# Block-sparse attention with two expert layers on one core: the first batch's attention drains in three steps, four output tiles are begun between them, and the token weights are made early

## The chip, the cores and the metric

The kernel runs on one core of a Trainium2 chip. The metric is the device time of one execution in microseconds (us), the median of several runs. Engines: PE is TensorE (its weight loads stand apart as PEld), DVE is VectorE, ACT is ScalarE, POOL is GpSimd, SP is the sync engine, which issues every DMA of this kernel.

## The reference

```python
# attention: q, k, v are [2, 8, 576, 64]; heads 0-3 see the last 32 positions, heads 4-7 see
# the earlier positions with the same remainder modulo 32
scores = scale * q @ k.T, masked to -1e9; attn = softmax(scores); attn_out = attn @ v
x = attn_out.transpose(0, 2, 1, 3).reshape(1152, 512)
# first expert layer: p = domain_probs / (domain_probs.sum(-1) + 1e-9), 4 experts, d_ff 1024
x = sum over e of p[:, e] * (relu(x @ w1[e]) @ w2[e])
# second layer, d_ff 1536, with weights in float64
out = (sigmoid(x @ w_gate) * (x @ w_val)) @ w_out
```

## The kernel before

**Attention** is cut into 32 groups, 16 for each of the two batches: 8 strided groups ("s", heads 4-7) and then 8 local ones ("l", heads 0-3). The text calls the first batch's groups 0 to 15 and the second's 16 to 31. A group passes through stages, one after the other: `scores` (TensorE, a mask product `sps` and the products of k and q into a score bank), `exp` (VectorE takes the negated maximum `nm`, ScalarE makes the exponentials `P` with their sums `sm`), `norm` (two small VectorE instructions on `sm`, then a multiplication of `P` on GpSimd), `transpose` (TensorE `tps`, VectorE copy `PT`), `values` (TensorE `o`, for two groups together) and `split` (the result is cut into a rounded part `xh` and a rest `xl`, the inputs of the next layer). `STAGES` says how many steps behind its scores a stage of a group stands: norm 1, transpose 3, values and split 5 (some 6). A step of `attention()` issues what falls on it, always in the order values, transpose, scores, exp, norm, split. All engines run their instructions in the order in which the program issues them.

The first batch's scores take steps 0 to 15. `DRAIN = 5` steps follow in which only its late stages are left, then the second batch begins at step 21. The first `FIRST_GROUPS = 21` steps run before the first expert layer; the steps after them are called from within its matrix products, 0.36 of a step for each product pair (`ATT_RATE`). In steps 12 to 20 the split reads the PSUM bank directly and VectorE makes both `xh` and `xl`; in other steps ScalarE copies the bank to `of` and GpSimd makes `xl` from that copy.

**Expert 0, "early"**: `early_up(s, T)` and `early_down(s, T)` work on 384 tokens in float32, each weight being split in two (`wh` by ScalarE, `wl` by GpSimd, one row of 128 each by `prep_early`, from a loaded tile `raw`), with three products for each pair. One call of `early_step` does one half of one such row, in this order: cast row, subtract row, and so on; the fifth call is the first on the item's second `raw` tile, the ninth ends an item. There are four items: up and down weights of the two halves of expert 0. `early_up(0, 0)` needs `xh` and `xl` of the first 384 tokens: rows 2 and 3 come from strided groups, rows 0 and 1 from local ones. `head_start(fb)` begins output tile `fb` of `early_up(0, 0)` with rows 2 and 3 (6 products); before the change that is done for tiles 0 and 1 in steps 17 and 18.

PSUM has four general banks (`gp`, "g"), three score banks (`sp_`, "s") and one for values (`op_`, "o"). `keep_warm(n)` issues n matrix products on zeros (`warm`), in the steps that `EMPTY` lists. `token_weights()` makes p from domain_probs on VectorE (in step 18); `spread_token_weights()` (step 19) transposes it on TensorE (`pps`), copies it out (`ptokT`), writes it to DRAM (`pd`) and reads it back spread over all partitions (`p00`). SP's queue is in the order of the program: the loads of later steps (`load_local(1)`, `load_strided_v(1, ...)`, `load_vl(1)`, `load_raw_to(n)`) stand behind one another.

After the early part come the experts 1 to 3 and the second layer, in float16 halves.

Of the kernel before, what the change touches and what calls it, by code (L numbers as in the profile page):

```python
# [9 lines left out]
F32 = mybir.dt.float32  # L10
# [24 lines left out]
WARM = 11  # L35
EMPTY = {0: 2, 1: 4, 2: 2, 3: 2, 4: 2, **{i: 2 for i in range(5, 16, 2)}, 16: 1, 19: 1, 20: 1}
T_BUFS = 4
# [9 lines left out]
QUAD = 4  # L47
FIRST_GROUPS = 21
PT_BUFS = 5
WEIGHTS_FROM = 12  # L50
DRAIN = 5
HEAD_START = (17, 18)
ATT_RATE = 0.36
# [53 lines left out]
def attn_moe_glu_kernel(ctx, tc, q, k, v, dp, w1, w2, wg, wv, wo, out):  # L107
# [20 lines left out]
    drp = ctx.enter_context(tc.tile_pool(name="drp", bufs=1, space=bass.MemoryType.DRAM))  # L128
    pd = drp.tile([NTB * E, 128], F32, tag="pd", name="pd")
    parked = {}  # L130
# [120 lines left out]
    zero = nc.const_aps.tensor(0.0, (128, 1), F32).bitcast(BF16)[:, 0:1]  # L251
    ptok = const.tile([128, NTB, E], F32, tag="ptok", name="ptok")
    psums = const.tile([128, NTB], F32, tag="psums", name="psums")
    SX = NI
# [35 lines left out]
    def token_weights():  # L290
        dve.tensor_reduce(psums, ptok, AX.X, ALU.add)
        dve.tensor_scalar(psums, psums, 1e-9, None, ALU.add)
        dve.reciprocal(psums, psums)
        dve.tensor_tensor(ptok, ptok, psums.unsqueeze(2).to_broadcast([128, NTB, E]), ALU.mult)

    def spread_token_weights():
        ps = gp.tile([128, 512], F32, tag="g", name="pps")
        nc.tensor.transpose(ps[:NTB * E, :128], ptok.rearrange("p t e -> p (t e)"), ident)
        t = atp.tile([128, 288], F32, tag="PT", name="ptokT", bufs=PT_BUFS)
        ptokT = t[:NTB * E, :128]  # L300
        dve.tensor_copy(ptokT, ps[:NTB * E, :128])
        nc.sync.dma_start(pd, ptokT)
        load_p(0, 0, p00)
# [3 lines left out]
    def load_p(e, T, t):  # L307

        m = TC // 128
        src = pd.rearrange("(t e) p -> e t p", e=E)[e, m * T:m * T + m, :]  # L310
        nc.sync.dma_start(t, bass.AP(src.tensor, src.offset, [[0, 128], [E * 128, m], [1, 128]]))
        pb[e, T] = t.rearrange("p a b -> p (a b)")
# [438 lines left out]
    def group_transpose(g):  # L751
        pp, _, n, w, m = soft.pop(g)
        ps = gp.tile([128, 512], F32, tag="g", name="tps")
        pv_ = ps[:w, :m * n].rearrange("p (a b) -> p a b", b=n)
        for j in range(m):
            nc.tensor.transpose(pv_[:, j, :], pp[:, j, :], ident[:n, :n])  # L756
        t = atp.tile([128, 288], F32, tag="PT", name="PT", bufs=PT_BUFS)
        tt = t[:w, :m * n].rearrange("p (a b) -> p a b", b=n)
        dve.tensor_copy(tt, pv_)
        pt_tiles[g] = tt  # L760

    def group_values(g):

        kind, b, c, half, hh = g
        if hh == 0:
            return
        if half and (kind, c) == ("l", 1):
            o = gp.tile([128, 512], F32, tag="g", name="o")
        else:
            o = op_.tile([128, 512], F32, tag="o", name="o")  # L770
        tts = [pt_tiles.pop((kind, b, c, half, x)) for x in range(2)]
        m, n = tts[0].shape[1], tts[0].shape[2]
        for j in range(m):
            for x in range(2):
# [7 lines left out]
                )  # L782
        if at_step[0] in range(WEIGHTS_FROM, FIRST_GROUPS):
            of_tiles[g] = o, o
            return
# [3 lines left out]

    def group_split(g):  # L790

        kind, b, c, half, hh = g
        if hh == 0:
            return
        o, of = of_tiles.pop(g)
        low = dve if of is o else pool_
        if kind == "s":
            kk = 2 + c
            hv, ov = (t[:, :288].rearrange("p (a u) -> p a u", u=NU) for t in (o, of))
            for T, off, s0, n in x_parts(b, 0, S):  # L800
                u0, u1 = s0 // 8, (s0 + n) // 8
                sel = lambda t: t[T][:, kk, off:off + n].rearrange("p (u a z) -> p z a u", a=4, z=2)[:, half]
                dve.tensor_copy(sel(xh), hv[:, :, u0:u1])
                low.tensor_tensor(sel(xl), ov[:, :, u0:u1], sel(xh).bitcast(F32), ALU.subtract)
        else:
            for T, off, s0, n in x_parts(b, 288 * half, 288 * half + 288):
                p0 = s0 - 288 * half
                dh, dl = xh[T][:, c, off:off + n], xl[T][:, c, off:off + n]
                dve.tensor_copy(dh, o[:, p0:p0 + n])
                low.tensor_tensor(dl, of[:, p0:p0 + n], dh.bitcast(F32), ALU.subtract)  # L810

    at_step = [0]

    def attention():
# [12 lines left out]
        step_of = [x + DRAIN * (x // (n // B)) for x in range(n)]  # L827
        at_stage = {}
        for name, behind in STAGES:
            for x in range(n):  # L830
# [6 lines left out]
                else:  # L837
                    at_stage[name, step_of[x] + behind] = gs[x]
        qk_strided(0, 0, (0,))
        for i in range(step_of[-1] + STAGES[-1][1] + 1):  # L840
            at_step[0] = i
            for name, _ in STAGES:
                if (name, i) in at_stage:
                    stage[name](at_stage[name, i])
            if i == 0:
                qk_strided(0, 0, (1,))
            if i in HEAD_START:
                head_start(HEAD_START.index(i))
            if i in EMPTY:
                keep_warm(EMPTY[i])  # L850
            for b in range(B):
                at = i - step_of[b * n // B]
                if b and at in (-5, -3):
                    qk_strided(b, 0, (int(at == -3),))
                if at in (2, 3):
                    qk_strided(b, 1, (at - 2,))
                if at in (6, 7, 9):
                    qk_local(b, (6, 7, 9).index(at))
            yield i
# [383 lines left out]
    with tc.manual_schedule():  # L1243
        load_strided_qk(0, 0)
        load_strided_qk(0, 1)
        warm_up()
        make_constants()
        load_local(0)
        load_strided_v(0, 0)
        load_strided_v(0, 1)  # L1250
        load_vl(0)
        nc.sync.dma_start(ptok, dp.rearrange("(t p) e -> p t e", p=128))
        for T in range(NT - 1):
            alloc_x(T)

        def attend():

            i = next(att, None)
            if i == 0:
                load_strided_qk(1, 0)  # L1260
                load_raw_to(2)
            if i == 6:
                load_raw_to(3)
                load_strided_qk(1, 1)
            if i == 9:
                load_strided_v(1, 0)
            if i == 11:
# [3 lines left out]
            if i == 18:  # L1271
                token_weights()
            if i == 19:
                spread_token_weights()
            if i == 20:
                load_vl(1)
# [3 lines left out]
        for i in range(FIRST_GROUPS):  # L1280
            attend()
            for _ in range((i >= WEIGHTS_FROM) + (i > 15)):
                early_step(0)
        n_none, n_step = 0, [0]
        halves = job(x_half())
# [21 lines left out]
        for n, u in enumerate(units):  # L1307
# [33 lines left out]
            for y in unit_steps(u):  # L1341
                if n < N_EARLY:
                    if y is None:
                        n_none += ATT_RATE
                        while n_none >= 1:
                            attend()
                            n_none -= 1
                        n_step[0] += 1
                        if n_step[0] % 2:
                            early_step(n)  # L1350
                elif y == "evac":
                    one_on()
# [36 lines left out]
```

## Time and profile before

| | us |
|---|---|
| median of 3 runs | 650.82 (650.52 to 651.32) |
| profiled execution | 651.06 |
| its span, first to last instruction | 648.9 |
| PE busy in the span | 638.2 (98%) |
| PEld, DVE, ACT, POOL busy | 469.3, 440.3, 341.7, 265.5 |
| granted TensorE clock, mean | 1.000 |

The span is 2.1 us shorter than the execution's time, which also holds what lies before the first and after the last instruction. A busy share counts the time in which an instruction of the engine runs; two instructions that overlap in the pipeline are counted once. Matrix products on zeros count as busy.

### The profile page before, as it was taken

The page shows a single profiled execution, that of the slowest core. Times are in us where ns is not written, and L with a number is a line of the kernel's source. Part 1 is how long each engine was busy: PE and PEld are TensorE (multiplying, and loading weights), DVE is VectorE, ACT ScalarE, POOL GpSimd, SP SyncE. Part 2 cuts the span into 40 slices and gives each one's busy share as a digit, 9 for nine tenths or more (in the row PEclk, how much of TensorE's full clock was granted, in tenths as well). Part 3 has the DMA queues.
Part 4 walks back from the last instruction along what each step waited for, and adds up shares of the span by engine and source line. Part 5 has one row for each costly group of instructions (what it writes and reads, how often), then busy time and mean ns, then how long its engine had stood idle before and what let it go on. Part 6 is the DMA issues. An engine that isn't in the chain of part 4 may idle for free.

```text
span 648.9 us, 12702 instructions
## 1 busy us (share of the span) xinstructions
PE 638.2 (98%) x4899; PEld 469.3 (72%) x4904; DVE 440.3 (68%) x885; ACT 341.7 (53%) x807; POOL 265.5 (41%) x307
## 2 busy tenths in 40 slices
PE   8889999999999999999999999999999999999998
PEld 5668889999676666666666666666979877987794
DVE  4876586787461886693887788898866659633432
ACT  5747553554854646774645554642565574532230
POOL 3665561000422226361335335440465377453540
PEclk9999999999999999999999999999999999999999
DMA  9965141030421544251664464354113832330002
GB/s 184 243 172 141 35 117 43 1 115 17 142 86 57 158 147 159 81 182 59 183 255 143 163 227 147 98 162 146 35 34 117 286 142 81 107 132 1 33 19 97
DMA packets 48884, 77.00 MB, mean 119 GB/s; under 512 B 19540, under 2 KB 24440, under 8 KB 47672
## 3 DMA queue, kind: packets, MB, share of 16 engines
q1 hardware_dynamic: 48824, 76.20, 37.6%
q8 instruction: 38, 0.62, 0.4%
q14 instruction: 22, 0.18, 0.1%
HBM read 59.66 MB, written 16.53 MB: 117 GB/s over the span
## 4 chain that ended last, share of the span: by engine, by line
PE 94%; DVE 1%; DMA 1%; SPq 1%; ACT 1%; issue 0%; POOL 0%; POOLq 0%; ACTq 0%
PE gps L874 23%; PE gps L876 23%; PE gps L875 23%; PE gps L976 19%; SPq L173 1%; PE sps L730 1%; PE warm L264 1%; PE tps L756 1%; PE o L780 1%; DMA ks<-in_k_dram 1%; ACT P L101 1%; DMA kl<-in_k_dram 1%; PE qkps L698 0%; PE qkps L676 0%; PE sps L717 0%; DVE nm L101 0%
## 5 line engine op out<-in xcount | busy, mean ns | idle before, releaser
L101 POOL TENSOR_TENSOR hl<-t,hh 128x384 f16<-128x384 f32 x72 | 76.5, 1065 | 179.2 <-ACT t L101 175.4
L976 PEld LDWEIGHTS <-w 128*128 128x128 f16 x1512 | 125.0, 98 | 1.8
L976 PE MATMUL gps<-x,w 128*128 128x192 f16 x1512 | 126.2, 246 | 0.0
L874 PE MATMUL gps<-x,w 128*128 128x384 f16 x288 | 93.9, 326 | 0.0
L875 PE MATMUL gps<-x,w 128*128 128x384 f16 x288 | 93.9, 326 | 0.0
L876 PE MATMUL gps<-x,w 128*128 128x384 f16 x288 | 93.9, 326 | 0.0
L874 PE MATMUL gps<-hh,w 128*128 128x384 f16 x288 | 93.9, 326 | 0.0
L875 PE MATMUL gps<-hl,w 128*128 128x384 f16 x288 | 93.9, 326 | 0.0
L876 PE MATMUL gps<-hh,w 128*128 128x384 f16 x288 | 93.9, 326 | 0.0
L874 PEld LDWEIGHTS <-w 128*128 128x128 f16 x576 | 56.4, 98 | 37.3 <-issue 0.2
L876 PEld LDWEIGHTS <-w 128*128 128x128 f16 x576 | 56.4, 98 | 37.2
L875 PEld LDWEIGHTS <-w 128*128 128x128 f16 x576 | 56.4, 98 | 36.4
L101 ACT ACTIVATE hh<-gps 128x384 f16<-128x384 f32 (+1 forms) x96 | 46.8, 487 | 48.8 <-PE gps L876 48.5
L101 POOL TENSOR_TENSOR stage<-magn,stage 128x512 f16<-128x512 f32 x36 | 45.5, 1273 | 45.1 <-ACT magn L101 38.9
L101 ACT ACTIVATE w<-raw,up 128x512 f16<-128x512 f32 x48 | 32.0, 715 | 34.8 <-DVE up L101 34.7
L101 ACT ACTIVATE P<-sps,nm 72x72 f32<-72x72 f32 (+1 forms) x112 | 36.4, 333 | 23.8 <-DVE sm L101 17.0
L101 ACT ACTIVATE bits<-raw 128x512 f32<-128x512 f32 x36 | 24.3, 674 | 38.1 <-DVE magn L101 37.9
L101 DVE SCALAR_TENSOR_TENSOR w<-raw,up,w 128x512 f16<-128x512 f32 x48 | 40.1, 871 | 5.1 <-ACT w L101 4.9
L101 POOL TENSOR_TENSOR sg<-four,sg 128x384 f32<-128x384 f32 x9 | 9.6, 1069 | 80.8 <-DVE four L101 77.9
L874 PE MATMUL gps<-w,hh 128*128 128x512 f16 (+1 forms) x112 | 41.6, 371 | 0.0
L875 PE MATMUL gps<-w,hh 128*128 128x512 f16 (+1 forms) x112 | 41.6, 371 | 0.0
L876 PE MATMUL gps<-w,hl 128*128 128x512 f16 (+1 forms) x112 | 41.6, 371 | 0.0
(145 smaller groups left out, 1281.5 us busy)
## 6 DMA issues: line engine op xcount, KB each, us to landing
raw<-in_moe_w_dram SPq DMA_DIRECT2D x32, 512.0 KB
raw<-in_moe_w_gate_dram SPq DMA_DIRECT2D x12, 512.0 KB
raw<-in_moe_w_val_dram SPq DMA_DIRECT2D x12, 512.0 KB
raw<-in_moe_w_out_dram SPq DMA_DIRECT2D x12, 512.0 KB
wg<-stage SPq DMA_DIRECT2D x21, 256.0 KB
wv<-stage SPq DMA_DIRECT2D x21, 256.0 KB
w<-wg SPq DMA_DIRECT2D x3, 1024.0 KB
wo<-stage SPq DMA_DIRECT2D x12, 256.0 KB
```

The source lines that it names most:

```text
L101: return f(*a, **k)
L173: nc.sync.dma_start(t[:, :, j, :], src[b, 2 * j:2 * j + 2].rearrange("h s d -> (h s) d").rearrange("(c p) d -> p c d", p=128),)
L264: nc.tensor.matmul(ps, zero.to_broadcast([128, 128]), zero.to_broadcast([128, 512]), start=True, stop=True,)
L730: nc.tensor.matmul(pv_[:, j, :], qs_, ks_, start=False, stop=j == m - 1)
L756: nc.tensor.transpose(pv_[:, j, :], pp[:, j, :], ident[:n, :n])
L780: nc.tensor.matmul(o[x * 64:x * 64 + 64, j * n:(j + 1) * n], lhsT, tts[x][:, j, :], start=True, stop=True)
L874: nc.tensor.matmul(ps, ah, bh, start=first and i == 0, stop=False)
L875: nc.tensor.matmul(ps, ah, bl, start=False, stop=False)
L876: nc.tensor.matmul(ps, al, bh, start=False, stop=last and i == n - 1)
L976: nc.tensor.matmul(o, l_, r_, start=first and x + kk + y == 0, stop=last and x * kk * y == 2, skip_group_check=True)
```

## The change

- The first batch drains in three steps: `DRAIN` is 3 and `FIRST_GROUPS` 19, so that the second batch begins at step 19. Group 11's values and split move from step 17 to 16, group 14's transpose from 17 to 16, group 15's from 18 to 17, and the values and splits of groups 14 and 15 from 19 and 20 to 18, both together. In steps 16 to 18 the transposes and values use the score banks.
- `head_start` runs for all four tiles, in steps 14, 15, 16 and 17.
- `split` from the PSUM bank is left to step 18 alone; steps 12 to 17 copy with ScalarE and subtract on GpSimd.
- The weight splits of item 0's first two rows move from steps 12 to 15 to steps 6 to 9; steps 16 to 18 do two calls each; from then on 0.55 call for each product pair (before 0.5).
- `token_weights` moves to step 3, in another layout of tokens, with its load at the front of SP's queue; `spread_token_weights` needs no transpose now and stands at step 9, ahead of `load_strided_v(1, 0)`.
- The first `raw` tile is loaded ahead of `load_strided_v(0, ...)`, `load_vl(0)` comes after the loads of step 0, and `load_vl(1)` comes at step 18.
- The transposes of the second batch's first q and k (`qk_strided(1, 0)`) move from steps 16 and 18 to 11 and 13; the last part of `qk_local` from the batch's step 9 to its step 8.
- Of the products on zeros those of steps 15, 16, 19 and 20 go (two, one, one and one).
- The banks that values use outside the drain are chosen by another rule.

```diff
-EMPTY = {0: 2, 1: 4, 2: 2, 3: 2, 4: 2, **{i: 2 for i in range(5, 16, 2)}, 16: 1, 19: 1, 20: 1}
+EMPTY = {0: 2, 1: 4, 2: 2, 3: 2, 4: 2, **{i: 2 for i in range(5, 14, 2)}}
-FIRST_GROUPS = 21
+FIRST_GROUPS = 19
-WEIGHTS_FROM = 12
-DRAIN = 5
-HEAD_START = (17, 18)
+EARLY_STEPS = {6: 1, 7: 1, 8: 1, 9: 1, 16: 2, 17: 2, 18: 2}
+EARLY_RATE = 0.55
+DRAIN = 3
+HEAD_START = {14: (0,), 15: (1,), 16: (2,), 17: (3,)}
...
-    pd = drp.tile([NTB * E, 128], F32, tag="pd", name="pd")
+    pd = drp.tile([E, NTOK], F32, tag="pd", name="pd")
...
-        dve.tensor_tensor(ptok, ptok, psums.unsqueeze(2).to_broadcast([128, NTB, E]), ALU.mult)
+        dve.tensor_tensor(
+            ptok_e, ptok.rearrange("p t e -> p e t"), psums.unsqueeze(1).to_broadcast([128, E, NTB]), ALU.mult)
     def spread_token_weights():
-        ps = gp.tile([128, 512], F32, tag="g", name="pps")
-        nc.tensor.transpose(ps[:NTB * E, :128], ptok.rearrange("p t e -> p (t e)"), ident)
-        t = atp.tile([128, 288], F32, tag="PT", name="ptokT", bufs=PT_BUFS)
-        ptokT = t[:NTB * E, :128]
-        dve.tensor_copy(ptokT, ps[:NTB * E, :128])
-        nc.sync.dma_start(pd, ptokT)
+        nc.sync.dma_start(pd.rearrange("e (p t) -> p e t", t=NTB), ptok_e)
         load_p(0, 0, p00)
...
     def group_transpose(g):
-        ps = gp.tile([128, 512], F32, tag="g", name="tps")
+        if FIRST_GROUPS - DRAIN <= at_step[0] < FIRST_GROUPS:
+            ps = sp_.tile([128, 512], F32, tag="s", name="tps")
+        else:
+            ps = gp.tile([128, 512], F32, tag="g", name="tps")
...
     def group_values(g):
-        if half and (kind, c) == ("l", 1):
+        if FIRST_GROUPS - DRAIN <= at_step[0] < FIRST_GROUPS:
+            o = sp_.tile([128, 512], F32, tag="s", name="o")
+        elif (half if kind == "s" else c) and (b == 0 or kind == "l" and half):
             o = gp.tile([128, 512], F32, tag="g", name="o")
...
-        if at_step[0] in range(WEIGHTS_FROM, FIRST_GROUPS):
+        if at_step[0] == FIRST_GROUPS - 1:
             of_tiles[g] = o, o
             return
...
     def attention():
+        m = n // B
+        for name, x, i in (("values", m - 5, m), ("split", m - 5, m), ("transpose", m - 2, m), ("transpose", m - 1, m + 1),
+                           ("values", m - 2, m + 2), ("values", m - 1, m + 2), ("split", m - 2, m + 2), ("split", m - 1, m + 2)):
+            at_stage = {k_: g for k_, g in at_stage.items() if k_[0] != name or g != gs[x]}
+            moved.append((name, i, gs[x]))
...
-                if b and at in (-5, -3):
-                    qk_strided(b, 0, (int(at == -3),))
+                if b and at in (-8, -6):
+                    qk_strided(b, 0, (int(at == -6),))
...
-                if at in (6, 7, 9):
-                    qk_local(b, (6, 7, 9).index(at))
+                if at in (6, 7, 8):
+                    qk_local(b, at - 6)
...
         load_strided_qk(0, 1)
+        nc.sync.dma_start(ptok, dp.rearrange("(p t) e -> p t e", t=NTB))
...
         load_local(0)
+        load_raw_to(1)
         load_strided_v(0, 0)
         load_strided_v(0, 1)
-        load_vl(0)
-        nc.sync.dma_start(ptok, dp.rearrange("(t p) e -> p t e", p=128))
...
             if i == 0:
                 load_strided_qk(1, 0)
+                load_vl(0)
                 load_raw_to(2)
+            if i == 3:
+                token_weights()
...
             if i == 9:
+                spread_token_weights()
                 load_strided_v(1, 0)
...
             if i == 18:
-                token_weights()
-            if i == 19:
-                spread_token_weights()
-            if i == 20:
                 load_vl(1)
...
         for i in range(FIRST_GROUPS):
             attend()
-            for _ in range((i >= WEIGHTS_FROM) + (i > 15)):
+            for _ in range(EARLY_STEPS.get(i, 0)):
                 early_step(0)
...
-                        n_step[0] += 1
-                        if n_step[0] % 2:
+                        n_step += EARLY_RATE
+                        while n_step >= 1:
                             early_step(n)
+                            n_step -= 1
```

## Rows read from the trace of the kernel before

**Rows 1.** Stretches of the start: us, busy per engine (count), TensorE clock, DMA share, GB/s.
```profile
0.00:13.20 13.20, 11.97 (x98) 6.91 (x99) 5.03 (x18) 6.56 (x31) 4.82 (x17) 1.00 0.88 177
13.20:32.70 19.50, 17.32 (x218) 12.65 (x220) 16.04 (x54) 15.51 (x82) 11.53 (x18) 1.00 1.02 238
32.70:44.40 11.70, 8.71 (x94) 6.96 (x95) 10.07 (x30) 6.09 (x20) 9.69 (x10) 1.00 0.84 208
44.40:55.40 11.00, 10.47 (x93) 9.32 (x92) 5.53 (x18) 5.99 (x30) 3.63 (x4) 1.00 0.73 186
55.40:75.00 19.60, 18.97 (x181) 16.59 (x181) 13.01 (x38) 13.47 (x64) 10.76 (x13) 1.00 0.18 56
75.00:600.00 525.00, 525.00 (x3831) 382.95 (x3830) 372.15 (x704) 283.96 (x564) 208.06 (x226) 1.00 0.36 118
```

**Rows 2.** TensorE in order of time: start, us, what [idle before <- releaser].
```profile
22.16 0.60 PE L264 MATMUL warm<-const-float32-0.0 128*128 128x512 bf16 x2
22.60 0.49 PE L698 MATMUL qkps<-ident,ql 128*128 128x128 f32 x3
...
31.79 0.90 PE L730 MATMUL sps<-klT,qlT 64*96 64x128 f32 x12
...
34.95 0.47 PE L756 MATMUL tps<-ident,P 96*128 96x96 f32 x3 [0.72 <-POOL P L101]
...
38.85 0.47 PE L756 MATMUL tps<-ident,P 96*128 96x96 f32 x3 [0.42 <-POOL P L101]
39.10 0.42 PE L874 MATMUL gps<-xh,wh 128*128 128x384 f32 x1
...
40.24 0.41 PE L676 MATMUL qkps<-ident,qs 72*128 72x72 f32 x4
...
43.15 0.27 PE L298 MATMUL pps<-ident,ptok 128*36 128x128 f32 x1 [1.26 <-DVE ptok L101]
43.34 0.72 PE L780 MATMUL o<-PT,vl 128*64 128x96 f32 x12
...
44.38 0.53 PE L874 MATMUL gps<-xh,wh 128*128 128x384 f32 x1
```

**Rows 3.** VectorE in order of time, same columns.
```profile
34.97 0.17 DVE L101 TENSOR_SCALAR sm<-sm 96x3 f32<-96x3 f32 x1
...
36.52 1.07 DVE L101 TENSOR_SCALAR sm<-sm 96x3 f32<-96x3 f32 x1
...
42.00 1.00 DVE L101 TENSOR_TENSOR ptok<-ptok,psums 128x36 f32<-128x36 f32 x1
```

**Rows 4.** GpSimd in order of time.
```profile
36.29 1.28 POOL L101 TENSOR_TENSOR wl<-raw,wh 128x512 fp32r<-128x512 f32 x1
```

**Rows 5.** Groups by shape, 13.2 to 44.4 us: count | busy us, mean ns | idle before.
```profile
L101 ACT ACTIVATE P<-sps,nm 96x128 f32<-96x128 f32 x24 | 8.5, 359 | 4.1 <-DVE sm L101 3.1 <-DVE nm L101 1.0
L101 POOL TENSOR_TENSOR P<-P,sm 96x384 f32<-96x384 f32 x8 | 6.6, 822 | 4.7 <-DVE sm L101 1.6 <-ACT P L101 1.0 <-ACT wh L101 1.0
...
L101 DVE TENSOR_REDUCE nm<-sps 96x3 f32<-96x384 f32 x8 | 4.4, 548 | 0.6 <-PE sps L730 0.5
...
L101 DVE COPY PT<-tps 128x288 f32<-128x288 f32 x8 | 3.6, 452 | 0.4 <-PE tps L756 0.2
...
L101 POOL TENSOR_TENSOR xl<-of,xh 128x192 fp32r<-128x192 f32 x3 | 2.1, 690 | 0.0
```

**Rows 6.** The sync engine's DMA issues in order of time.
```profile
10.62 1.72 SPq L166 DMA_DIRECT2D vs<-in_v_dram  x2
...
37.60 4.08 SPq L240 DMA_DIRECT2D raw<-in_moe_w_dram  x2
44.33 0.33 SPq L302 DMA_DIRECT2D pd<-ptokT  x1
45.70 0.37 SPq L311 DMA_DIRECT2D p<-pd  x1
```

**Rows 7.** ScalarE in order of time.
```profile
43.21 0.62 ACT L101 CAST wh<-raw 128x512 fp32r<-128x512 f32 x1 [1.08 <-DMA raw<-in_moe_w_dram]
```

More of the change, by code (lines that the diff above doesn't have):

```diff
@@ L252, in attn_moe_glu_kernel @@
     ptok = const.tile([128, NTB, E], F32, tag="ptok", name="ptok")
+    ptok_e = const.tile([128, E, NTB], F32, tag="ptok_e", name="ptok_e")
     psums = const.tile([128, NTB], F32, tag="psums", name="psums")
@@ L307, in load_p @@
     def load_p(e, T, t):
-        m = TC // 128
-        src = pd.rearrange("(t e) p -> e t p", e=E)[e, m * T:m * T + m, :]
-        nc.sync.dma_start(t, bass.AP(src.tensor, src.offset, [[0, 128], [E * 128, m], [1, 128]]))
+        src = pd[e, T * TC:(T + 1) * TC]
+        nc.sync.dma_start(t.rearrange("p a b -> p (a b)"), bass.AP(src.tensor, src.offset, [[0, 128], [1, TC]]))
         pb[e, T] = t.rearrange("p a b -> p (a b)")
@@ L788, in group_values, with group_split @@
         of_tiles[g] = o, of
-    def group_split(g):
-        kind, b, c, half, hh = g
-        if hh == 0:
+    def group_split(*gs):
+        for kind, b, c, half, hh in gs:
+            break
+        else:
             return
-        o, of = of_tiles.pop(g)
-        low = dve if of is o else pool_
         if kind == "s":
[L798 to L804, printed above, removed]
-        else:
[L806 to L810, printed above, removed]
+            parts = x_parts(b, 0, S)
+        else:
+            parts = x_parts(b, 288 * half, 288 * half + 288)
+        tiles = [of_tiles.pop(g) for g in gs]
+        for T, off, s0, n in parts:
+            for g, (o, of) in zip(gs, tiles):
+                low = dve if of is o else pool_
+                if kind == "s":
+                    kk, u0, u1 = 2 + g[2], s0 // 8, (s0 + n) // 8
+                    sel = lambda t: t[T][:, kk, off:off + n].rearrange("p (u a z) -> p z a u", a=4, z=2)[:, half]
+                    src = lambda t: t[:, :288].rearrange("p (a u) -> p a u", u=NU)[:, :, u0:u1]
+                else:
+                    p0 = s0 - 288 * half
+                    sel = lambda t: t[T][:, g[2], off:off + n]
+                    src = lambda t: t[:, p0:p0 + n]
+                dve.tensor_copy(sel(xh), src(o))
+                low.tensor_tensor(sel(xl), src(of), sel(xh).bitcast(F32), ALU.subtract)
     at_step = [0]
@@ L827, in attention @@
         step_of = [x + DRAIN * (x // (n // B)) for x in range(n)]
-        at_stage = {}
+        at_stage, moved = {}, []
         for name, behind in STAGES:
@@ L844, in attention @@
                     stage[name](at_stage[name, i])
+                both = [g for name_, i_, g in moved if (name_, i_) == (name, i)]
+                if name == "split":
+                    group_split(*both)
+                else:
+                    for g in both:
+                        stage[name](g)
             if i == 0:
                 qk_strided(0, 0, (1,))
-            if i in HEAD_START:
-                head_start(HEAD_START.index(i))
+            for fb in HEAD_START.get(i, ()):
+                head_start(fb)
             if i in EMPTY:
@@ L1281, in attn_moe_glu_kernel @@
             attend()
-            for _ in range((i >= WEIGHTS_FROM) + (i > 15)):
+            for _ in range(EARLY_STEPS.get(i, 0)):
                 early_step(0)
-        n_none, n_step = 0, [0]
+        n_none, n_step = 0, 0
         halves = job(x_half())
```

## The prediction

> **What bounds the kernel now.** I read the busy time by stretches first. From 75 us on TensorE is busy in every microsecond: 525.00 of 525.00 [rows 1]. Whatever the change does, it does in the first 75 us; a microsecond won there moves all the rest forward by a microsecond, and nothing behind can win it again. There TensorE is idle 1.2 us up to 13.2 us, 2.2 us up to 32.7, 3.0 us in the drain up to 44.4, 0.5 us up to 55.4 and 0.6 us up to 75 [rows 1]: 7.5 us in all, beside products on zeros that are no use to the result. So the account is: time won = TensorE's idle time removed + useless products removed - new idle time.
>
> Then TensorE in order of time [rows 2]. The scores of groups 14 and 15 begin at 31.79 and last 0.90 us; I call their end S = 32.7. `early_up(0, 0)` begins at T0 = 44.38. The reader is to see what lies in these 11.7 us: transposes that wait for GpSimd's `P` (0.72 and 0.42), two head starts, the second batch's `qkps`, products on zeros, and 1.26 us of waiting for the token weights (`ptok`) ahead of a transpose, with the last `values` queued behind it at 43.34. The VectorE rows say why the weights were late: that multiplication of 36 elements took 1.00 us [rows 3].
>
> **What is removed.** Products on zeros run 0.22 us apart (22.16, then 22.60 after two of them) [rows 2]; five go: 1.1 us. `pps` goes: 0.2 us to the row behind it [rows 2], with its 1.26 us of waiting, its copy, and on VectorE some 1.6 us between S and T0 (three small instructions and the 1.00). The two `qkps` pairs (0.25 a set of four by their spacing, four sets, 1.0 us) leave the drain but reappear before S.
>
> **The new drain, added up from S.** One head start takes 1.14 us (39.10 to 40.24), one set of `values` 0.7, one of `tps` 0.25 (38.85 to 39.10) [rows 2]. Four heads, four `values` (10, 11, 14, 15) and four `tps` (12 to 15) are 4.6 + 2.8 + 1.0 = 8.4 us of TensorE: the lower bound. Waits on top, by the order within the steps, with `nm` 0.55, `PT` 0.45, three exponentials 1.1, `P` on GpSimd 0.82 [rows 5] and 0.35 for the two `sm` instructions (one is 0.17 [rows 3]): head 0 ends at S + 1.15, `values` 10 at 1.85, `tps` 12 at 2.1. `PT` 12 and `nm` 15 follow on VectorE to 3.15, exponentials 15 to 4.3. `sm` 14 stands behind `nm` 15, so `P` 14 is ready at 4.4. TensorE does head 1, `values` 11 and `tps` 13 to 4.2, waits 0.25, then does `tps` 14 and head 2, to 5.85. `sm` 15 stands behind `PT` 13 and 14 on VectorE, to 5.5; GpSimd is free of `xl` 10 by 5.3 and gives `P` 15 at 6.45. TensorE waits 0.65, does `tps` 15, head 3 and both `values`, to 9.3. The first split must be made before row 0 of tile 0 can go on: S + 9.5. So T0 comes 11.7 - 9.5 = 2.2 us sooner after S, and two more heads (2 x 1.14 = 2.3 us) are done by then: 4.5 us. The bounds are 8.4 (no wait: 5.6 us won) and 11.7 (waits as before: 2.3 us won).
>
> **S itself moves.** Four parts, none of which the trace shows as it will be. (1) One `raw` tile of 0.5 MB now stands ahead of `load_strided_v(0, 0)`, whose issue was at 10.62 [rows 6], with the DMA engines at a share of 1.02 and 238 GB/s [rows 1]: 2.2 us later. How long before its use the load had landed isn't shown, so the wait at the first `values` lies between 0 and 2.2; I take 0.7, since `values` of step 7 has no wait before. (2) Two `wl` subtractions of 1.28 us [rows 4] go to steps 7 and 9, each behind the split's two `xl` (0.69 [rows 5] and less) and ahead of the next `norm`: between 0 and 2.6 us; I take 0.6, as GpSimd is busy only 11.5 of 19.5 us there [rows 1]. (3) The `qkps` in steps 11 and 13 add 1.0 us on TensorE and 0.9 on VectorE, which has 3.5 us to spare over the stretch [rows 1], and the token weights 0.7 at step 3; TensorE's own waits take up part: +0.3 (0 to 1.0). (4) VectorE sheds group 7's `xl` in step 13 (two instructions, some 0.8 us) and the last local transposes come a step sooner: -0.6 (-1.0 to 0). Sum: S is 1.0 us later, with bounds of -1.0 and +5.8.
>
> **After T0.** `early_up(0, 0)` now has 8 product pairs instead of 12, so only 4 calls of the weight split fall into it. The down weights of item 1 lack three half rows when `early_down(0, 0)` starts, and they are issued there in one go: two `wl` in a chain (1.28 each [rows 4]) behind casts on ScalarE. The products reach the last of them some 2.0 us after the start and it is ready after 2.9: 0.9 us of new waiting (0 to 2.5). SP's queue has changed too: `p00` is read back only when `pd` has landed; that took 1.4 us (44.33 to 45.70 [rows 6]) and now stands at step 9, ahead of all later loads. I put the hold at 2 us. The second `raw` tile of item 1 then lands near 45.2, since before it was issued at 37.60 [rows 6] and ScalarE waited for it until 43.21 [rows 7]; the cast of it is wanted about T0 + 5 = 48. It is hidden, with 3 us to spare. The tile behind it waits for `load_vl(1)`, which waits for group 15's `values`: +0.2 (0 to 2). The 1.1 us of idle time up to 75 us I leave as they are (gone at best).
>
> The Trainium skill's "DMA: Bandwidth & Descriptors", section "Anatomy of one DMA", says that a semaphore wait for a DMA is made on the issuing sequencer and that most of a DMA's fixed time, about 2.0 us, lies behind the last byte. The 1.4 us from `pd` to `p` [rows 6] agree; by the page's figure the hold would be 2 us and more, the landing of the `raw` tile still before its use, and the sum the same.
>
> **Sum.** -2.2 (drain) - 2.3 (two heads) + 1.0 (S) + 1.1 (after T0) = -2.4 us. The useless products and the transpose are in the drain's 2.2 already. The profiled execution is 651.06 with a span of 648.9 and stands 0.24 above the median of 650.82; I take the difference from the median: 648.4.
>
> **Rivals.**
> (a) *The drain closes well and S holds*: VectorE, busy 10.1 of the drain's 11.7 us [rows 1], is the true pace before S too, and shedding three `xl` and two copies moves S forward or leaves it. Then -5.6 or so at best for drain and heads, 0 for S, 0.5 behind: some -5, 645.8. For it: from 31 us VectorE hardly rests. Against: the waits for `P` in [rows 2] are GpSimd's.
> (b) *Moved GpSimd work blocks VectorE, no change.* A `sm` of 0.17 us took 1.07 at 36.52 while GpSimd ran a `wl` from 36.29 to 37.57 [rows 3, 4]. Five GpSimd jobs (two `wl`, three splits) now fall in steps 7 to 16, among twenty such small instructions. If each job holds one `sm` up by half to all of its time, S is 2.5 to 3.5 us later instead of 1.0, and 0.5 more is lost in the drain: 0 to +0.5 in place of -2.4, thus 650.5. The Trainium skill's "SBUF — State Buffer", section "SBUF: two separate sides", states it as a rule: VectorE in a two-port mode and GpSimd exclude one another for a whole instruction. The row agrees, and it speaks against moving work to GpSimd.
> (c) *Slower: late weights.* Place: SP's queue from step 9 on. If the hold at `p00` grows with everything queued ahead of it, the second `raw` tile of item 1 lands after 48 and `early_down(0, 0)` waits a microsecond for each one later; the next tile, behind `load_vl(1)`, holds ScalarE up, and with it the exponentials. It decides from a landing at 50.5 on (2.4 us past need); at 53 it gives +2, 652.6. For it: the DMA engines are busy all the time up to 44 us (0.84 in the drain [rows 1]). Against: total bytes hardly change, and token weights now come in larger pieces.
>
> **How the numbers follow.** No change means within 0.2%, 1.3 us, about what runs of this kernel can tell. Forecast 48% (own range 646.8 to 650.0, 46 of the 48 faster by more), (a) 17%, (b) 21% (of it 18 same), (c) 14%. Faster: 46 + 17 + 1 = 64%; same: 2 + 18 + 2 = 22%; slower: 2 + 12 = 14%. The range takes (a) down to 645.8 and (b) whole, and (c) up to 651.4: about 80%.
>
> **What would show it.** T0 (first `gps<-xh,wh` after the four heads) near 43 instead of 44.4, no `pps`, idle time of TensorE between S and T0 of about 1.1 us. S near 33.7; a wait of TensorE at the first `o<-PT,vs`; `wl` in steps 7 and 9 with a `sm` of over 0.5 us beside it. A wait of `gps<-hh,wl` for GpSimd at the start of `early_down`. `p` issued long after `pd`. A granted clock of 1.00 throughout as in [rows 1], though there are fewer products on zeros; a drop to half would be a cost that I give no room. The prediction is wrong if S moves by more than 2.5 us or if stretches behind 75 us are no longer full.

## The result and the profile after

| | before | after |
|---|---|---|
| median | 651.04 us (650.33 to 651.49, 15 executions) | 655.85 us (651.22 to 658.59, 15 executions) |
| ratio | 1 | 1.0059, 95% interval 1.0036 to 1.0083 |
| profiled execution, its span | 651.06, 648.9 | 657.12, 655.3 |
| mean granted clock in it | 1.000 | 0.992 |

The kernel became slower, where 2.4 us less was forecast. The executions of the kernel after are spread over 7 us, and they are ordered by their mean granted clock: 651.22 to 652.2 in the five at 0.999 to 1.0, 654.21 to 655.85 at 0.995 to 0.997, 656.33 to 658.59 at 0.987 to 0.992. Of the 103 executions of the kernel before whose clock is on record, taken beside the experiments below, 101 are at 0.999 or 1.0 and two (652.52 and 653.42) at 0.997.

The stretches of [rows 1] in the profile after, the last one cut at 102 us (columns as there):

```profile
0.00:13.20 13.20, 11.78 (x100) 6.92 (x103) 5.00 (x18) 6.52 (x31) 4.80 (x17) 1.00 0.76 164
13.20:32.70 19.50, 14.66 (x181) 10.96 (x186) 16.08 (x48) 14.28 (x72) 11.02 (x16) 0.98 0.95 226
32.70:44.40 11.70, 11.48 (x84) 9.13 (x83) 5.36 (x19) 4.49 (x22) 4.36 (x7) 0.59 0.83 157
44.40:55.40 11.00, 10.04 (x96) 8.65 (x97) 5.60 (x18) 5.08 (x20) 6.89 (x7) 1.00 0.61 137
55.40:75.00 19.60, 17.33 (x169) 14.78 (x168) 11.95 (x33) 13.68 (x62) 12.63 (x13) 1.00 0.32 107
75.00:102.00 27.00, 25.93 (x233) 22.04 (x232) 18.28 (x54) 15.38 (x67) 15.61 (x22) 1.00 0.23 77
102.00:600.00 498.00, 498.00 (x3584) 359.44 (x3583) 356.95 (x666) 271.37 (x517) 195.98 (x210) 1.00 0.37 121
```

From 13.2 to 32.7 us TensorE now does 14.7 us of work instead of 17.3. From 32.7 to 44.4 it looks fuller than before (11.48 of 11.70 us), but the clock column reads 0.59: the same products take longer. From 44.4 to 102 us 4.3 us are idle. TensorE in order of time, the rows that answer to [rows 2]:

```profile
19.70 0.72 PE L782 MATMUL o<-PT,vs 72*64 72x72 f32 x16 [1.38 <-DMA vs<-in_v_dram]
...
31.35 0.47 PE L756 MATMUL tps<-ident,P 96*128 96x96 f32 x3 [1.60 <-POOL P L102]
31.66 0.50 PE L714 MATMUL sps<-ml,identb 96*96 96x384 bf16 x2
...
39.91 0.69 PE L890 MATMUL gps<-xh,wh 128*128 128x384 f32 x1
40.39 0.52 PE L891 MATMUL gps<-xl,wh 128*128 128x384 f32 x1
40.71 0.52 PE L892 MATMUL gps<-xh,wl 128*128 128x384 f32 x1
...
43.32 0.33 PE L891 MATMUL gps<-xl,wh 128*128 128x384 f32 x1
43.49 0.34 PE L892 MATMUL gps<-xh,wl 128*128 128x384 f32 x1
...
49.35 1.21 PE L782 MATMUL o<-PT,vl 128*64 128x96 f32 x24
50.52 0.42 PE L890 MATMUL gps<-xh,wh 128*128 128x384 f32 x1
...
59.34 0.47 PE L673 MATMUL qkps<-ident,qk 72*128 72x72 f32 x4 [1.38 <-DVE hl L102]
...
61.87 0.44 PE L892 MATMUL gps<-hh,wl 128*128 128x384 f32 x1 [0.45 <-POOL wl L102]
```

The first product of head 0 (39.91) stands right behind the last scores and so marks S; the `gps` behind the double `values` (50.52) is T0. At 40.4 two products stand 0.32 us apart, at 43.3 two of the same shape 0.17: half the rate and the full one. Short stretches show where it changes:

```profile
30.00:32.00 2.00, 0.65 (x5) 0.43 (x5) 1.93 (x9) 0.79 (x5) 1.20 (x3) 1.00 0.81 171
32.00:34.00 2.00, 2.00 (x19) 1.64 (x20) 1.02 (x4) 0.65 (x4) 1.56 (x3) 0.50 0.25 33
...
42.00:44.00 2.00, 2.00 (x21) 1.76 (x21) 0.69 (x2) 0.40 (x1) 0.00 (x0) 0.94 1.04 198
```

The clock goes from 2.4 to 1.2 GHz (1.00 to 0.50) at 32, 0.7 us behind the end of the wait of 1.60 us, and back at 42, some 10 us later.

What lay behind that wait: VectorE ([rows 3] before), then GpSimd in the same time ([rows 4]):

```profile
14.05 0.21 DVE L102 TENSOR_TENSOR ptok_e<-ptok,psums 128x36 f32<-128x36 f32 x1
...
23.81 1.25 DVE L102 TENSOR_SCALAR sm<-sm 72x4 f32<-72x4 f32 x1
25.09 0.17 DVE L102 RECIPROCAL sm<-sm 72x4 f32<-72x4 f32 x1
...
28.27 1.83 DVE L102 TENSOR_SCALAR sm<-sm 96x3 f32<-96x3 f32 x1
30.14 0.17 DVE L102 RECIPROCAL sm<-sm 96x3 f32<-96x3 f32 x1
```

```profile
23.77 1.26 POOL L102 TENSOR_TENSOR wl<-raw,wh 128x512 fp32r<-128x512 f32 x1
...
27.77 1.08 POOL L102 TENSOR_TENSOR xl<-of,xh 128x192 fp32r<-128x192 f32 x2
28.81 1.27 POOL L102 TENSOR_TENSOR wl<-raw,wh 128x512 fp32r<-128x512 f32 x1
```

The addition of 1e-9 to three sums begins while GpSimd runs `xl` and ends 0.02 us after the `wl` behind it: 28.27 + 1.83 against 28.81 + 1.27. The reciprocal behind it, the `P` of `norm` on GpSimd and the transpose at 31.35 all wait in turn, and then the clock falls. The first held addition (23.81, 1.25 us) ends 0.03 us behind the `wl` of 23.77.

SP's issues ([rows 6] before):

```profile
26.44 0.49 SPq L300 DMA_DIRECT2D pd<-ptok_e  x1
33.94 0.36 SPq L308 DMA_DIRECT2D p<-pd  x1
...
42.88 0.37 SPq L241 DMA_DIRECT2D raw<-in_moe_w_dram  x1
```

### The profile page after: what moved, and what is told of

The parts are those of the page before. It is cut to its first block, busy times and chain, and to the rows that moved or that the text cites. A ratio compares the mean times of both kernels' runs of the same rounds, so it can differ in the third digit from the quotient of the medians.

```text
span 655.3 us, 12689 instructions
## 1 busy us (share of the span) xinstructions
PE 641.3 (98%) x4893; PEld 471.7 (72%) x4898; DVE 438.7 (67%) x880; ACT 342.8 (52%) x810; POOL 268.3 (41%) x311
## 4 chain that ended last, share of the span: by engine, by line
PE 92%; DVE 2%; SPq 2%; POOL 2%; DMA 1%; issue 1%; ACT 0%; POOLq 0%
PE gps L890 23%; PE gps L892 23%; PE gps L891 22%; PE gps L992 19%; PE o L782 1%; PE tps L756 1%; PE sps L727 1%; SPq L174 1%; DMA vs<-in_v_dram 1%; DVE sm L102 1%; POOL wl L102 1%; POOL P L102 1%; DVE nm L102 0%; PE sps L714 0%; SPq L159 0%
## 5 line engine op out<-in xcount | busy, mean ns | idle before, releaser
L102 POOL TENSOR_TENSOR P<-P,sm 72x288 f32<-72x288 f32 (+1 forms) x32 | 23.8, 743 | 44.0 <-DVE sm L102 41.2
```

Of the source, the lines that this page charges most:

```text
L102: return f(*a, **k)
```

## The experiments

Theory after this profile: late work ahead of S (`vs` behind a `raw` tile, `sm` held by GpSimd) and the clock that falls behind its waits are the loss. Rivals: another wait takes the place of any one repaired; the loss lies behind T0; SP's hold does it. Where a run leaves out the 1e-9, the term makes no difference to the result, since each sum is at least 1. Below, "full clock" is a mean granted clock of at least 0.999 in an execution.

**1. Fill the waits.** Twenty more products on zeros, which do no useful work.

```diff
-EMPTY = {..., **{i: 2 for i in range(5, 14, 2)}}
+EMPTY = {..., **{i: 2 for i in range(5, 14, 2)}, 5: 6, 6: 6, 8: 3, 11: 9}
```

> The changed kernel with 4 more products on zeros at the end of step 5, 6 more after step 6, 3 more after step 8 and 7 more after step 11, where TensorE waited 1.07, 1.38, 0.63 and 1.60 us. Theory (the waits before S let TensorE's clock fall, and the fall is what makes most executions 654 to 658 us): clock 1.00 in every execution, times near 651.3 with a spread under 1 us, as the undisturbed executions of the changed kernel have. Rival (the lost time is late weights and the hold of SP's queue, the clock is a side effect): times stay at 654 to 658, or rise by the 4 us of added products.

Measured: 652.84 us (651.99 to 657.5, 11), ratio 1.0036 (1.0022 to 1.005); nine of the eleven at full clock. Its stretch and its head 0:

```profile
13.20:32.70 19.50, 18.87 (x205) 12.81 (x207) 16.33 (x49) 14.38 (x74) 10.82 (x15) 1.00 0.91 216
```

```profile
36.80 0.45 PE L890 MATMUL gps<-xh,wh 128*128 128x384 f32 x1
37.08 0.34 PE L891 MATMUL gps<-xl,wh 128*128 128x384 f32 x1
```

More work and, by the medians, 3.0 us less time (by the ratios 1.5 us, with intervals that overlap). With the order of the executions above, this shows the fall of the clock to be a part of the loss. Head 0 is still 4.1 us later than S of before, at the full clock, so it isn't all: neither the theory's 651.3 nor its spread of under 1 us came. The drain, with its additions, takes 9.60 us here (T0 at 46.40).

**2. `vs` first.** Only the order of two loads on SP.

```diff
-        load_raw_to(1)
         load_strided_v(0, 0)
         load_strided_v(0, 1)
+        load_raw_to(1)
```

> The changed kernel with its first raw tile loaded behind the two loads of v again instead of ahead. Theory (the raw tile makes the first values wait 1.4 us): the wait of o<-PT,vs for the DMA is gone, S comes 1 to 1.4 us sooner, and the clock falls less often: median 649.5 to 653. Rival (the wait merely hides the stall of VectorE behind GpSimd that follows): the wait goes, the stalls of sm grow by as much, S stays where it is, median 654 to 656.

Measured: 656.03 us (651.13 to 661.31, 12), 1.0075 (1.0041 to 1.011). The wait of 1.38 for `vs` is gone and nothing is won: the 1.60 for `P` stands (now at 30.58), head 0 comes at 39.71, and five of the twelve are at 0.982 to 0.984, lower than any of the kernel after. The place of head 0 says little by itself, as TensorE's first product of k and q (`sps<-ksT,qsT`) comes 0.8 us later in this profile (7.19 against 6.38).

**3. No held addition, and both repairs.**

```diff
-        dve.tensor_scalar(sm, sm, 1e-9, None, ALU.add)
```

> The changed kernel without the addition of 1e-9 to the softmax sums (left out: that term of the denominator), so one small VectorE instruction fewer in each group, the one that was seen to last 1.25 and 1.83 us beside GpSimd's wl. Theory (those two stalls are GpSimd's hold on VectorE, and they set S): the stalls of 1.1 and 1.7 us go, the waits of tps for P of 1.6 us go, S comes 1.5 to 3 us sooner, median 649 to 652. Rival (the next small instruction, the reciprocal, is held up in its place): the reciprocal lasts over 1 us at the same places, S gains 0.3 us at most, median 654 to 656.

> The changed kernel with both edits: the raw tile behind the loads of v, and no addition of 1e-9. Theory (these two waits are all that the change costs before S): clock 1.00 in every execution, S near 34, median 647.5 to 649.5, faster than the kernel before, as the sum of the prediction had it. Rival (the drain itself or the weights behind it give the gain back): S near 34 and still 650.5 or more.

Measured, without the addition: 650.99 us (648.84 to 653.64, 12), 1.0006 (0.9993 to 1.0019), four at full clock (648.84 to 650.17). TensorE in its profile, head 0 and then the end of the drain:

```profile
34.76 0.44 PE L889 MATMUL gps<-xh,wh 128*128 128x384 f32 x1
...
43.03 1.21 PE L781 MATMUL o<-PT,vl 128*64 128x96 f32 x24
44.20 0.42 PE L889 MATMUL gps<-xh,wh 128*128 128x384 f32 x1
```

S to T0 is 9.44 us, and the clock is at 1.00 up to 52 us; behind the bank wait of 1.37 us (53.03) it falls here too. All reciprocals of `sm` take 0.16 to 0.17. Six of those up to 72 us begin while a GpSimd job runs, and none is held, so the expectation's rival is out. With `vs` first as well: 654.1 us (648.93 to 657.48, 12), 1.0046 (1.0017 to 1.0075); head 0 comes at 33.31 and T0 at 42.76, 1.4 us better still, but a bank wait of 1.37 us behind T0 (51.59) is followed by half clock from about 53 to 60, and half of the executions are at 0.986 or 0.987. In the profiled execution (650.96, at 0.995) the gain ahead of T0 is given back behind it. Where the clock falls in those six no profile shows.

The same line left out of the kernel before, as a control:

> The kernel before, without the addition of 1e-9 (left out). It tells how much of the repaired kernels' gain is the change's own. Theory (the stalls of sm cost the kernel before little, as only one of about 1 us stands there, in the drain): 650.0 to 650.7. Rival (each of the 32 small instructions lay on the path): 648 to 649, as fast as the repaired change.

Measured: 649.75 us (648.7 to 652.89, 12), 0.9996 (0.9983 to 1.0009): 1.1 us below the median of before on the same chip (650.89), with five of twelve now at 0.994 to 0.997, against none of the 26 of the kernel before beside it. Even there one instruction less makes a full clock less sure; why, no run shows.

**4. The wait behind T0.** Four begun tiles hold all four general banks; the second batch's last early transpose waits for one. It goes to the bank of the values instead (on top of the version without the addition).

```diff
-                ps = gp.tile([128, 512], F32, tag="g", name="qkps")
+                if (b, c, nm) == (1, 1, "ks"):
+                    ps = op_.tile([128, 512], F32, tag="o", name="qkps")
+                else:
+                    ps = gp.tile([128, 512], F32, tag="g", name="qkps")
```

> The changed kernel without the addition of 1e-9 (left out), and with the transposes of the second batch's second k (the set that waited 1.37 us) going to the bank of the values instead of a general bank. Theory (the four begun tiles hold the general banks; that wait both costs its 1.4 us and lets the clock fall behind it): the wait goes, executions at full clock come to 647.3 to 648.0 (before this edit 648.84), and fewer executions show a clock under 1.00, median 648 to 650. Rival (something else, such as the weight splits on GpSimd, is late next at the same place): the wait of qkps goes and gps<-hh,wl waits for GpSimd by as much, 648.8 at full clock.

Measured: 651.84 us (648.73 to 656.25, 12), 1.0016 (0.9996 to 1.0037), inconclusive in time. The bank wait is gone, and TensorE waits three times for the weight split instead, 1.63 us. That is the rival's outcome, and so are the three executions at full clock (648.73 to 649.36). Behind these short waits the clock falls as well, to 0.50 from 56 to 59 us:

```profile
52.35 0.44 PE L894 MATMUL gps<-hh,wl 128*128 128x384 f32 x1 [0.56 <-POOL wl L102]
...
53.78 0.44 PE L894 MATMUL gps<-hh,wl 128*128 128x384 f32 x1 [0.62 <-POOL wl L102]
...
55.02 0.45 PE L894 MATMUL gps<-hh,wl 128*128 128x384 f32 x1 [0.45 <-POOL wl L102]
```

**5. Two attempts that failed or half failed.** All repairs so far with five more products on zeros:

> The changed kernel with every repair so far: no addition of 1e-9 (left out), the raw tile behind the loads of v, the bank of the values for that one transpose, and five more products on zeros (two more in step 5, three more in step 11). Theory: all waits over 0.6 us before 60 us gone, clock 1.00 in nearly every execution, median 647 to 648.3, faster than the kernel before by 0.3 to 0.5%. Rival (the clock falls for another reason than these waits): still executions at 654 and more.

Measured: 655.17 us (651.69 to 661.85, 8), 1.0066 (1.0036 to 1.0097), none at full clock. ScalarE's cast waits 3.34 us for the first `raw` tile, up to 21.74, and TensorE waits 1.79 us at 23.80 for `klT` behind that. With the same order of loads the cast began at 19.27 without a wait in experiment 3. And the first item's splits four steps later (`EARLY_STEPS` 10 to 13 in place of 6 to 9), nothing else:

> The changed kernel, with nothing changed but the steps of the first four calls of the weight split: 10 to 13 instead of 6 to 9, so that the two wl run on GpSimd in steps 11 and 13. Theory (a wl directly ahead of a norm holds VectorE's sm for its whole length wherever it stands): the stalls of sm move from the two steps to later ones, or shrink if VectorE comes to its sm elsewhere in time; S within 1 us of the changed kernel's, median 653 to 656.5. Rival (the two steps chosen are the bad place, as the split's two xl stand there too): S 2 us sooner, median 650 to 653.

Measured: 652.69 us (652.0 to 655.36, 7), 1.0032 (1.002 to 1.0045). Six of seven are at full clock, head 0 comes at 34.99, but its last product waits 1.17 for `wl` in the drain: a steady loss for an unsteady one. The time is the rival's, but the theory's mechanism is there: the holds have moved with the two `wl`. VectorE, then GpSimd:

```profile
30.98 1.21 DVE L102 TENSOR_SCALAR sm<-sm 96x3 f32<-96x3 f32 x1
...
35.56 1.71 DVE L102 TENSOR_SCALAR sm<-sm 96x3 f32<-96x3 f32 x1
```

```profile
30.90 1.26 POOL L102 TENSOR_TENSOR wl<-raw,wh 128x512 fp32r<-128x512 f32 x1
...
36.00 1.26 POOL L102 TENSOR_TENSOR wl<-raw,wh 128x512 fp32r<-128x512 f32 x1
```

Each ends within 0.03 us of its `wl`, and at the old places the addition takes 0.15 to 0.31.

**6. SP's hold.** `spread_token_weights` at step 18, ahead of `load_vl(1)`, nothing else.

> The changed kernel with one edit: the writing and reading back of the token weights at step 18 instead of 9. SP's queue then isn't held for 7.5 us between them. Theory (the hold is hidden: no wait of TensorE in the changed kernel's trace names a transfer of later steps): full-clock executions at 651 to 652, the same as the changed kernel's, and as many with a fallen clock. Rival (the hold starves the weight split): full-clock executions 1 us or more faster.

Measured: 654.72 us (650.35 to 658.75, 12), 1.0048 (1.0024 to 1.0072). The hold of 7.5 us (26.44 to 33.94) was hidden, but for a few tenths at most: only two executions are at full clock (650.35 and 651.08), and they are 0.1 and 0.9 below the fastest of the kernel after.

**7. Two begun tiles in place of four.** `HEAD_START = {15: (0,), 16: (1,)}`, nothing else.

> The changed kernel with two tiles begun (steps 15 and 16) instead of four. Theory (two more heads move 2.3 us of products into the drain, and then two general banks are missing behind it, which costs 1.4 us at the second batch's transposes): the wait of 1.38 us for a bank goes, the start of early_up comes up to 2.3 us sooner but with 12 products more to do; the two nearly cancel, full-clock executions at 650.5 to 652. Rival (begun tiles are the whole gain of the drain): 653 and more at full clock.

Measured: 653.21 us (649.54 to 655.0, 12), 1.0025 (1.0008 to 1.0043); at full clock 649.54 to 649.84 (three), against 651.22 and more with four, and below both expectations. Two more begun tiles, forecast at -2.3 us, cost 1.7. With two the transpose behind T0 waits 0.48 for `ksT` instead of 1.38 for a bank.

**8. The kernel before, fed.** Without the addition, and with eight more products on zeros (`EMPTY` 11: 4, 15: 4, 19: 5).

> The kernel before, without the addition of 1e-9 (left out) and with 8 more products on zeros (two more in step 11, two in step 15, four in step 19), at places where TensorE waited 0.45, 0.51 and 1.27 us. Theory (the executions of 651.3 to 652.9 without these products are those whose clock fell, and products in the waits keep it up): clock 0.999 or 1.00 in all executions, 649.0 to 650.3, median 649.6, faster than the kernel before by about 0.2%. Rival (the clock falls behind another wait, or the products cost what they save): executions over 651 remain, or all stand at 650.5 to 651.

Measured: 648.87 us (648.65 to 649.21, 5), 0.997 (0.9958 to 0.9981), all at full clock: faster than both kernels, with none of the change.

**9. The change repaired.** No addition, `vs` first, the bank, `EMPTY` 5: 4 and 11: 5, the token weights spread at step 18, and three, three and four early calls in steps 16 to 18.

> The changed kernel with all repairs: no addition of 1e-9 (left out), the raw tile behind the loads of v, the transpose into the bank of the values, five more products on zeros before step 12, the writing and reading back of the token weights at step 18 instead of 9, and ten calls of the weight split in steps 16 to 18 instead of six. Theory (S, the bank, the hold of SP's queue and the late weight split are all that took the gain): the waits for wl after the start of early_down go, executions at full clock come to 647 to 648, and fewer than half show a clock under 0.998; median 647.5 to 650. Rival (the drain's gain lies elsewhere, for instance in the batch's later steps): full-clock executions at 648.8 as all repaired ones so far.

Measured: 647.77 us (646.36 to 652.22, 6), 0.9954 (0.9938 to 0.9969). The waits for `wl` behind T0 are gone. Two of six are still below full clock; the profiled one (652.22) shows where, on ScalarE and then on TensorE:

```profile
21.22 0.62 ACT L102 CAST wh<-raw 128x512 fp32r<-128x512 f32 x1 [2.13 <-DMA raw<-in_moe_w_dram]
```

```profile
23.28 0.55 PE L698 MATMUL qkps<-ident,kl 128*128 128x128 f32 x3 [1.65 <-DVE klT L102]
```

The clock stands at 0.52 and 0.50 from 24 to 34 us behind it. So the four early calls go from steps 6 to 9 to steps 8 to 11, and the same with two begun tiles, to price these once more:

```diff
-EARLY_STEPS = {6: 1, 7: 1, 8: 1, 9: 1, 16: 3, 17: 3, 18: 4}
+EARLY_STEPS = {8: 1, 9: 1, 10: 1, 11: 1, 16: 3, 17: 3, 18: 4}
```

> The repaired version (no 1e-9 added to sm, which changes nothing in the output since the sums are at least 1; v loads ahead of the raw tile; ks in the bank of the values; seven more products on zeros in steps 5 and 11; token weights spread at step 18; ten early calls in steps 16 to 18) with the four early calls of steps 6 to 9 in steps 8 to 11, so that ScalarE's cast no longer waits 2.13 us for a raw tile that has not landed. Theory (the clock falls behind single waits; that wait was the last of them ahead of S): no execution below 0.997, qkps kl without its wait of 1.65, head 0 near S of 33 to 34, median 646.3 to 647.5. Rival (the stretch ahead of S is too thinly filled in this order, and any small wait lets the clock fall): a third or more of the executions at 0.992 or less as before, median 648 or more, and the fall starts at another wait.

> The same with only tiles 0 and 1 begun, in steps 15 and 16 (tiles 2 and 3 are then done whole in early_up(0, 0)). Theory (the prediction's term: each tile begun while the drain waits anyway takes 1.14 us out of the full stretch behind it, and the 1.4 us that four banks held cost is repaired): 1 to 2.5 us slower than the version with four tiles at the same clock, 647.5 to 649.5. Rival (the drain's waits are no longer there to be filled, so that the heads only move TensorE's work from behind T0 to ahead of it, as two tiles were 1.7 us faster than four in the unrepaired order): within 0.7 us of the version with four tiles at the same clock, or faster.

(The "seven more" products on zeros of the first expectation are the five named above.) Measured, four tiles: 647.32 us (646.81 to 651.19, 9), 0.9951 (0.9937 to 0.9966), eight of nine at full clock (one at 0.995, where none below 0.997 was expected). Its first two stretches ahead of and in the drain, and TensorE's head 0 and T0:

```profile
13.20:32.70 19.50, 18.36 (x227) 13.46 (x229) 14.42 (x46) 15.94 (x82) 12.73 (x18) 1.00 1.01 241
32.70:44.40 11.70, 10.93 (x105) 8.84 (x106) 6.12 (x20) 6.53 (x26) 8.54 (x11) 1.00 0.81 174
```

```profile
34.23 0.44 PE L892 MATMUL gps<-xh,wh 128*128 128x384 f32 x1
...
42.47 1.21 PE L784 MATMUL o<-PT,vl 128*64 128x96 f32 x24
43.64 0.41 PE L892 MATMUL gps<-xh,wh 128*128 128x384 f32 x1
```

The wait of 1.65 is gone, S to T0 is 9.41 us, and T0 stands 0.74 ahead of [rows 2]. Two tiles: 648.96 us (647.73 to 652.01, 12), 0.9979 (0.9965 to 0.9993), all at full clock: 1.6 us slower by the medians, 0.9 by the lowest. With the bank repaired, two more begun tiles are worth 0.9 to 1.6 of the 2.3 us.

## Why the prediction was wrong, step by step

The account of the profiled execution, by the prediction's own terms:

| term | forecast | measured in the profile after |
|---|---|---|
| S | +1.0 | +7.2 (39.91 against 32.7) |
| S to T0 | -2.2 (9.5 for 11.7) | -1.1 (10.6 for 11.7) |
| two more begun tiles | -2.3 | -2.3 as work; their cost is in the last row |
| after T0 | +1.1 | +2.2 (3.3 us idle up to 102 us against 1.2) |
| sum | -2.4 | +6.0 (657.12 - 651.06 = 6.1) |

**The step that failed is "S itself moves".** It was put at +1.0 and measured +7.2, beyond its own upper bound of 5.8. TensorE was busy 7.7 of the 7.9 us from 32.0 to 39.9 at half clock; at the full one that is, as an estimate, some 3.8 us less. So S moved by 3.4 us for the waits, and by 3.8 for the clock, which the sum had at nothing; experiment 1, at the full clock and with its waits filled, has 4.1 for the first. Of the drain 1.1 us more is the clock's, which leaves the forecast 9.5. Without the clock the sum is 3.4 - 2.2 - 2.3 + 2.2 = +1.1; the five executions at full clock stand 0.2 to 1.2 above before. That is no change or little more, the outcome of rival (b); the clock makes it the 4.8 us of the medians. (That rival's own terms give 650.8 to 651.3, and the +2 of (c) gives 652.8; the 650.5 and 652.6 set down for them are slips.) Both things that the prediction named as proving it wrong came: S moved by more than 2.5 us, and from 75 to 102 us TensorE is idle for 1.1 us.

*Part (1), `vs` behind a `raw` tile*: 1.38 measured, 0.7 taken of 0 to 2.2. Right in kind. Repaired alone it won nothing (experiment 2); with the additions gone it was worth 1.4 us of S (experiment 3). *Part (2), two `wl` ahead of `norm`*: 0.6 taken of 0 to 2.6; the two held additions lost 1.1 and 1.7 us against a `sm` of 0.15. The row that priced it was in front of me ([rows 3]: 1.07 instead of 0.17), and I put it into a rival at half and in the sum at less. GpSimd's idle time in the stretch, by which I chose the low value, is no measure: what counts is which VectorE instruction falls beside which job. The second addition was held over the end of an `xl` as well, so that the two lost 2.8 us together, more than the bound of 2.6. The Trainium skill's "SBUF — State Buffer", section "SBUF: two separate sides", the rule that I weighed as rival (b), agrees with the end of the 1.83 us 0.02 us after GpSimd's job. Experiment 3 and the moved `wl` of experiment 5 settle it: the holds go with the addition and move with `wl`, and with both parts repaired head 0 comes at 33.31, 0.6 us behind S of before. Those 0.6 are what is left for parts (3) and (4), forecast at -0.3; no run takes them apart.

**The clock was given no room.** I had noted five products on zeros as time won and a drop of the clock as a thing to watch, without a price. Experiment 1 gives a size: twenty more such products shortened the median by 3.0 us. What an added wait costs here is not its length alone. The Trainium skill's "TensorE: Matmul & The Clock Gate", part 1, says that the clock has two levels and follows how busy TensorE has lately been, and that it differs from run to run; the executions at 0.987 to 1.0 of one kernel agree.

**The drain was right.** It took 9.60 us at the full clock with the additions (experiment 1) and 9.44, 9.45 and 9.41 without them (experiments 3 and 9), against 9.5. Its two waits for `P` were 0.22 and 0.75 in experiment 1, forecast at 0.25 and 0.65. So the sum by instructions and their order held; that its `P` 15 should stand at 6.3 by its own terms, not 6.45, changes nothing. Rival (c) did not decide either: SP's hold was hidden, as forecast, though it was 7.5 us where 2 was taken (the 1.4 us of [rows 6], which the prediction calls in agreement with 2.0, were no guide to it).

**After T0**, the forecast late `wl` was there (0.45, and 1.63 in experiment 4), but ahead of it stood a wait that I had not looked for: who holds the banks that the begun tiles occupy. It is the second half of why two more tiles brought nothing (experiment 7) until it was repaired (experiment 9).

With all of this repaired the change brings what it was forecast to bring, or near it: 647.32, by the account -0.7 (T0) - 2.3 (tiles) - 0.3 (idle behind T0) = -3.3, measured -3.5 in the profiled execution. But that is not the forecast come true, since the repairs bring gains of their own: the fed kernel before, with none of the change, already had a ratio of 0.997 in experiment 8, against 0.9951 here. By these the plan itself is worth about 0.002, some 1.2 us and half of the forecast, and as the two intervals overlap, even that isn't shown.

**What stays open**: which wait lets the clock fall, and why the same kernel keeps it in one execution and not in the next. Most of the falls seen began behind single waits of 1.37 to 1.79 us, and one in experiment 4 and one in the first of experiment 5 behind three shorter ones for `wl` (0.45 to 0.64). But such waits did not always bring one (experiment 1 has the bank wait of 1.37 too and keeps 1.00 in its profile), and taking one of two away (experiment 2) gave deeper falls, not fewer. Nor is the clock all of the spread: the version with two tiles in experiment 9 ran from 647.73 to 652.01 without a fall. Two things differ between profiles that no run set on purpose: TensorE's first `sps<-ksT,qsT` comes at 5.76 to 7.19 us, so that places in two profiles compare to about a microsecond only; and with `vs` first, the `raw` tile that the first cast waits for landed at 20.41, 21.22 and 21.74, in one case by 19.27. Both profiles in which that cast held TensorE up began early (5.76 and 5.84), while the version with the later cast was profiled in an execution that began at 7.16. That the later cast helps to keep the clock up rests therefore on the executions (20 of 21 at full clock in the two versions with it, against four of six), not on the profile.

## What to carry to other kernels

Price a wait on TensorE in a thin stretch twice: once with its length, once with what follows at half clock, and put products on zeros or real work there before taking any away. When work moves to GpSimd, list the small VectorE instructions that will run beside it and charge each that a row has shown to be held (here the addition, not the reciprocal) up to the whole job; such an instruction, where it can be left out, is worth more there than its own length. When accumulation is begun early, follow each bank to the instruction that frees it, and ask who needs that bank next; repair one wait at a time but judge the set, since each repair here showed the next wait, and none of them alone came out faster than the kernel before, while the set did. And give the kernel before the same repairs, or the gain is credited to the wrong change.

## What the runs showed of the hardware

A `tensor_scalar` on 96x3 values was held up to 1.83 us in the profile after (1.99 in experiment 1), over the end of one GpSimd instruction to that of the next, while the reciprocals of the same tile kept their 0.16 to 0.17. The token weights' multiplication took 1.00 us in [rows 3] and 0.21 after, where no GpSimd job ran beside it (before, `wl` did; its layout changed too). A write to DRAM that is read back took 7.5 us on SP with the DMA engines at a share of 0.76 in that time, against 1.4 at 0.06 in [rows 6]. And one kernel's executions differ by up to 10 us (651.13 to 661.31 in experiment 2), nearly in the order of their granted clock.
